# Strassen's output layer: its sums and low halves moved from GpSimd to VectorE, in wider pieces, with the products in another order

## Chip, core and metric

The kernel runs on one core of one Trainium2 chip. The metric is the device time of one execution in microseconds (us), the median of several runs; less is better. An execution lasts 1.85 us longer than the span of its trace, which goes from the first to the last instruction.

## What is computed

Attention over 4 batches of 12 heads, 448 tokens and 64 dimensions, then a gated layer and a cosine layer, each followed by a matrix product. All inputs are float32.

```python
x = attention(q, k, v, g_q, g_k)               # 1792 tokens x 768
g = x @ w_gate                                 # 768 x 1536
x = (silu(g) * (x @ w_val)) @ w_out            # 1536 x 768
h = x @ w2_in                                  # 768 x 2048
out = (h * cos(h)) @ w2_out                    # 2048 x 768: the output layer
```

The change is in the last line's product, and in what prepares its weights.

## The kernel before

**Precision.** An fp32 factor is held as two float16 halves, high and low (the low half is the value less the high one), and a product of two such factors is three matmuls: high by high, high by low, low by high (`mm_out`).

**The output layer** multiplies A (1792 tokens by 2048) by w2_out with one level of Strassen's scheme in Winograd's form: seven products of blocks of half the tokens, half the inner dimension and half the columns, in place of eight. The inner half is cut in eight chunks c of 128 rows. `A[c]` is a tile with four places of 896 columns: A11 and A12 as float16 pairs, A21 and A22 as fp32 (`f32_of(c, 2)` and `f32_of(c, 3)`). The products also take sums of blocks: S3 = A11 - A21, S2 = A22 - S3, S4 = A12 - S2, S1 = A21 + A22. A product goes over four `runs`, each with two chunks and seven token tiles of 128, six matmuls of 128x384 for each tile and run: 42 matmuls in a run, 28 runs in the layer. The seven tiles lie in seven of eight PSUM banks, and products that share a sum go on accumulating in the same banks (a chain). `o_fin` takes a finished tile out of PSUM, scaled.

**The sums of blocks** are emitted behind each run for its two chunks: `s_32` (S3 into tiles of its own, S2 in A11's place, behind A11's run), `s_4` (S4 in A12's place, behind A12's), `s_22` (A22 split into halves in A11's place, behind S2's) and `s_1` (behind S3's). Each does 448 columns at a time. VectorE does the sums, ScalarE the high half (`put`), GpSimd the low half and one difference in `s_4`.

**The weights** of the layer are w2_out's blocks and their sums T. `pre_step` loads w2_out, turns it and stores it as `o32`. `t_step` loads a chunk of `o32` into a `raw` tile, does four subtractions of 384 columns on GpSimd and stores the result as `oT`; it is called late in the cosine layer (from chunk 5, batch 3) and at the output layer's start. `o_load` loads two chunks' weights for a run, `o_split` makes their halves (ScalarE the high one, VectorE the low one).

**The cosine layer** before it (called h here) has 8 chunks by 4 batches, 36 matmuls of 128x448 each; `fin_h` makes A's blocks of them, on VectorE and ScalarE with a small subtraction on GpSimd. Before h comes the gated layer's second product (out1), with `pre_step` beside it.

**Order.** All DMAs are issued from SyncE's queue (SP). Each engine works its own queue in order. A scheduler sets the order in these queues when the kernel is built; it moves an instruction of one part between those of another.

## Time and profile before

| | us |
|---|---|
| median of 3 runs (1327.07 to 1330.24) | 1329.25 |
| the profiled execution | 1329.15 |
| its span | 1327.3 |
| TensorE busy | 1182.5 |
| VectorE busy | 981.9 |
| ScalarE busy | 691.6 |
| GpSimd busy | 547.1 |

Busy times are sums over the whole span. Stages have different limits, so a stage is read by the busy time within it and by what each engine waited for there. A busy TensorE is not a TensorE at its peak: matmuls overlap, so a matmul's own duration is about twice the step from one to the next.

### The profile page before, as it was taken

What the parts mean: (1) busy time and instruction counts of PE and PEld (TensorE: products, weight loads), DVE (VectorE), ACT (ScalarE), POOL (GpSimd) and SP (SyncE); (2) the same over time, 40 slices, a digit from 0 to 9 for tenths busy, and PEclk for the clock granted to TensorE, in tenths of its full rate; (3) what the DMA queues carried; (4) which work ended last, traced back from release to release, by engine and by line L of the source; (5) the groups of instructions that cost most, each with busy time, mean ns of one, the idle gap of its engine ahead of it and who ended that gap; (6) DMA issues with size and microseconds to landing.
All of it is one profiled execution on the core that took longest, in us unless ns stands there. A gap on an engine that the chain in (4) does not pass through costs nothing. (4 is left out here: it accounts for less than half of the span.)

```text
span 1327.3 us, 18341 instructions
## 1 busy us (share of the span) xinstructions
PE 1182.5 (89%) x6292; PEld 661.4 (50%) x6292; DVE 981.9 (74%) x1760; ACT 691.6 (52%) x1342; POOL 547.1 (41%) x437
## 2 busy tenths in 40 slices
PE   1887988998999989999999999999999886648998
PEld 0332333444764459544586548555555443325665
DVE  5987866798779992478644986677788799989531
ACT  3675655544666544556643453577776554335210
POOL 7753402534324452145540125122215478889400
PEclk9898989998999999999999999999999998869999
DMA  5655666459877797787576977501123761121222
GB/s 147 173 149 134 184 170 178 99 162 253 240 213 188 224 234 232 186 212 188 123 232 227 307 284 260 170 0 48 48 72 127 256 236 60 36 65 49 72 67 71
DMA packets 220782, 211.54 MB, mean 159 GB/s; under 512 B 147601, under 2 KB 178193, under 8 KB 220689
## 3 DMA queue, kind: packets, MB, share of 16 engines
q1 hardware_dynamic: 220688, 210.38, 54.7%
q8 instruction: 49, 0.80, 0.3%
q14 instruction: 45, 0.36, 0.1%
HBM read 138.44 MB, written 41.57 MB: 136 GB/s over the span
## 5 line engine op out<-in xcount | busy, mean ns | idle before, releaser
L163 PE MATMUL mm<-xy,wp 128*128 128x448 f16 x2484 | 493.5, 355 | 6.3 <-DVE ga L1128 3.2
L163 PEld LDWEIGHTS <-wp 128*128 128x128 f16 x2880 | 278.4, 99 | 280.5 <-issue 36.6
L163 PE MATMUL mm<-g,wp 128*128 128x448 f32 x864 | 183.1, 369 | 1.6 <-DVE ga L1136 1.6
L163 POOL TENSOR_TENSOR g<-tmp,g 128x224 f16<-128x224 f32 (+1 forms) x112 | 112.1, 1010 | 159.1 <-ACT g L1257 154.5
L163 PEld LDWEIGHTS mm<-g,wp 128*128 128x128 f32 x864 | 160.6, 188 | 19.7 <-issue 4.4
L163 PEld LDWEIGHTS <-g 128*128 128x128 f16 x1008 | 99.9, 99 | 94.8 <-issue 27.2
L163 POOL TENSOR_TENSOR g<-ga,g 128x448 fp32r<-128x448 f32 x48 | 64.5, 1357 | 145.4 <-ACT g L1138 145.3
L507 ACT ACTIVATE pr<-s,sm,esc 128x448 f32<-128x448 f32 x84 | 60.3, 718 | 80.2 <-DVE sm L501 73.7
L163 PE MATMUL s<-T 128*64 128x448 f16 x336 | 63.8, 398 | 39.6 <-DVE T L666 21.6
L163 POOL TENSOR_TENSOR wp<-w,wp 128x768 fp32r<-128x768 f32 x36 | 72.3, 2011 | 60.5 <-ACT wp L1024 40.3
L163 PE MATMUL s<-wp,g 128*128 128x384 f16 x432 | 78.7, 338 | 14.6 <-ACT u L1361 9.7
L935 DVE TENSOR_SCALAR w<-raw 128x768 int32<-128x768 int32 x68 | 48.5, 716 | 53.1 <-POOL wp L163 19.4
L163 PE MATMUL mm<-wp,g 128*128 128x384 f16 x432 | 75.4, 327 | 10.5 <-DVE g L1253 4.3
L163 PEld LDWEIGHTS <-T 128*64 128x64 f16 (+1 forms) x432 | 28.8, 109 | 110.2 <-issue 83.6
L163 POOL TENSOR_TENSOR ri<-ss,half 128x14 f32<-128x14 f32 x24 | 64.1, 2672 | 37.9 <-DVE ss L356 36.3
L497 DVE TENSOR_REDUCE sm<-s 128x1 f32<-128x448 f32 x84 | 51.2, 615 | 36.4 <-PE s L163 36.3
L163 POOL TENSOR_TENSOR p<-pr,p 128x448 f16<-128x448 f32 x36 | 41.1, 1149 | 88.6 <-ACT p L531 70.5
L1342 DVE SCALAR_TENSOR_TENSOR wp<-w,oscl,wp 128x384 f16<-128x384 f32 x56 | 54.7, 1001 | 29.8 <-ACT wp L1341 29.7
L937 DVE SCALAR_TENSOR_TENSOR w<-raw,w 128x768 int32<-128x768 int32 x68 | 74.9, 1101 | 0.6
L936 DVE SCALAR_TENSOR_TENSOR w<-raw,w 128x768 int32<-128x768 int32 x68 | 74.1, 1093 | 0.6
L163 POOL TENSOR_TENSOR xy<-tmp,xy 128x448 f16<-128x448 f32 x24 | 27.8, 1160 | 110.2 <-ACT xy L774 83.4
L955 ACT ACTIVATE raw<-w 128x768 f32<-128x768 f32 x56 | 46.9, 838 | 47.6 <-DVE w L937 34.4
(199 smaller groups left out, 2108.3 us busy)
## 6 DMA issues: line engine op xcount, KB each, us to landing
raw<-in_moe_w_out_dram SPq DMA_DIRECT2D x28, 768.0 KB, 5.3
raw<-in_moe_w_in_dram SPq DMA_DIRECT2D x16, 768.0 KB, 5.5
raw<-in_moe_w_gate_dram SPq DMA_DIRECT2D x12, 768.0 KB, 6.2
raw<-in_moe_w_val_dram SPq DMA_DIRECT2D x12, 768.0 KB, 5.8
wp<-scr_gate SPq DMA_DIRECT2D x24, 384.0 KB, 4.5
w<-scr_out SPq DMA_DIRECT2D x24, 384.0 KB, 3.9
wp<-scr_val SPq DMA_DIRECT2D x24, 384.0 KB, 5.0
y<-tmp SPq DMA_DIRECT2D x30, 224.0 KB, 3.9
```

The source lines that it names most:

```text
L163: r = f(*args, **kw)
L497: nc.vector.tensor_reduce(sm[:, 0, t:t + 1], slot[n][:, :S], axis=AX.X, op=ALU.max)
L507: nc.scalar.activation(e, slot.pop(n)[:, :S], AF.Exp, bias=sm[:, 1, t:t + 1], scale=esc, accum_out=sm[:, 2, t:t + 1],)
L935: nc.vector.tensor_scalar(wi, hi, 3, 0x3FFFFFF8, op0=ALU.logical_shift_left, op1=ALU.bitwise_and)
L936: nc.vector.scalar_tensor_tensor(wi, hi, -0x40000000, wi, op0=ALU.bitwise_and, op1=ALU.bitwise_or)
L937: nc.vector.scalar_tensor_tensor(wi, lo, 29, wi, op0=ALU.logical_shift_right, op1=ALU.bitwise_or)
L955: nc.scalar.activation(sq_dst[0], w32, AF.Square, accum_out=n[:, 0:1])
L1342: nc.vector.scalar_tensor_tensor(wp[:, i, 1], w, so, wp[:, i, 0], op0=ALU.mult, op1=ALU.subtract)
```

## The change

Sums and low halves of the output layer go to VectorE, in pieces of 896 columns where their temporaries allow it (these are now `raw` tiles, two of them). S1's sum is taken in `s_4` and lands in A21's place. `s_1` follows S2's run. The products come in the order A11, A12, S3, S2, A22, S1, S4, with A22 in a chain of its own, and `o_fin` adds the results up in another way. `t_step` also goes to VectorE; it begins in the gated layer's second product (from visit `TSTEP` on), where it uses four small `yt` tiles, so its load and its store are four DMAs each of 192 KB, and it goes on in h, in a `raw` tile, with one load and four stores.

```diff
@@ -42,6 +42,7 @@
 NPH = 3
 EARLY = 75
 PREL = 33
+TSTEP = 25
 HPRE = (5, 3)
 LO = 3
 WL = 8
@@ -1044,18 +1045,25 @@
     t_new = []
     t_in = []
 
-    def t_step():
+    def t_step(more=True, small=None):
 
         if t_in:
             c, t = t_in.pop()
             for d, x, y in ((0, 1, 0), (1, 3, 1), (3, 3, 0), (2, 2, 3)):
-                gps.tensor_sub(t[:, d], t[:, x], t[:, y])
-            stores.append((oT[c].rearrange("p m f -> p (m f)"), t.rearrange("p m f -> p (m f)")))
-        if t_new:
+                nc.vector.tensor_sub(t[d], t[x], t[y])
+            stores.extend((oT[c][:, i], t[i]) for i in range(4))
+        if t_new and more:
             c = t_new.pop(0)
-            t = rot("raw").tile([P, 6 * 256], I32, tag="raw", name="raw").bitcast(F32)
-            sync.dma_start(t, o32[c].rearrange("p m f -> p (m f)"))
-            t_in.append((c, t.rearrange("p (m f) -> p m f", f=CO)))
+            w_store()
+            if small is None:
+                t = rot("raw").tile([P, 6 * 256], I32, tag="raw", name="raw").bitcast(F32)
+                sync.dma_start(t, o32[c].rearrange("p m f -> p (m f)"))
+                t = [t[:, i * CO:(i + 1) * CO] for i in range(4)]
+            else:
+                t = [small.tile([P, S], F32, tag="yt", name="yt")[:, :CO] for _ in range(4)]
+                for i in range(4):
+                    sync.dma_start(t[i], o32[c][:, i])
+            t_in.append((c, t))
         return bool(t_in or t_new)
 
     def pre_step(more=True):
@@ -1272,53 +1280,54 @@
 
     def put(dst, src):
         nc.scalar.activation(dst[0], src, AF.Copy)
-        gps.tensor_sub(dst[1], src, dst[0])
-
-    def pair(c, i, k):
+        nc.vector.tensor_sub(dst[1], src, dst[0])
+
+    def pair(c, i, k=slice(0, TS)):
         return A[c][:, i, 0, k], A[c][:, i, 1, k]
+
+    def wide_tmp():
+        return rot("raw").tile([P, 6 * 256], I32, tag="raw", name="raw").bitcast(F32)[:, :TS]
 
     def s_32(c):
 
         tt = nc.vector.tensor_tensor
         S3[c] = [s3_pool[0].tile([P, TS], F16, tag="s3", name="s3") for _ in range(2)]
-        for k in HALVES:
-            hi, lo = pair(c, 0, k)
-            s3, s2 = tmp(), tmp()
-            tt(s3, hi, f32_of(c, 2)[:, k], op=ALU.subtract)
-            tt(s3, s3, lo, op=ALU.add)
-            put([x[:, k] for x in S3[c]], s3)
-            tt(s2, f32_of(c, 3)[:, k], s3, op=ALU.subtract)
-            put((hi, lo), s2)
+        hi, lo = pair(c, 0)
+        s3, s2 = wide_tmp(), wide_tmp()
+        tt(s3, hi, f32_of(c, 2), op=ALU.subtract)
+        tt(s3, s3, lo, op=ALU.add)
+        nc.scalar.activation(S3[c][0], s3, AF.Copy)
+        tt(s2, f32_of(c, 3), s3, op=ALU.subtract)
+        nc.scalar.activation(hi, s2, AF.Copy)
+        tt(S3[c][1], s3, S3[c][0], op=ALU.subtract)
+        tt(lo, s2, hi, op=ALU.subtract)
 
     def s_4(c):
 
+        tt = nc.vector.tensor_tensor
         for k in HALVES:
             (h1, l1), (h2, l2) = pair(c, 1, k), pair(c, 0, k)
             s4, u = tmp(), tmp()
-            nc.vector.tensor_tensor(s4, h1, h2, op=ALU.subtract)
-            gps.tensor_sub(u, l1, l2)
-            nc.vector.tensor_tensor(s4, s4, u, op=ALU.add)
+            tt(s4, h1, h2, op=ALU.subtract)
+            tt(u, l1, l2, op=ALU.subtract)
+            tt(s4, s4, u, op=ALU.add)
             put((h1, l1), s4)
+        tt(f32_of(c, 2), f32_of(c, 2), f32_of(c, 3), op=ALU.add)
 
     def s_22(c):
 
-        for k in HALVES:
-            put(pair(c, 0, k), f32_of(c, 3)[:, k])
+        put(pair(c, 0), f32_of(c, 3))
 
     def s_1(c):
 
-        s1 = [tmp(), tmp()]
-        for k, t in zip(HALVES, s1):
-            nc.vector.tensor_tensor(t, f32_of(c, 2)[:, k], f32_of(c, 3)[:, k], op=ALU.add)
-        for k, t in zip(HALVES, s1):
-            put(pair(c, 3, k), t)
+        put(pair(c, 3), f32_of(c, 2))
 
     s3_pool = []
     u_pool = []
     out_w = {}
     out_wp = {}
 
-    CHAINS = ((("A11", 0), ("A12", 2)), (("S2", 7), ("S3", 5), ("A22", 6)), (("S1", 4), ("S4", 3)))
+    CHAINS = ((("A11", 0), ("A12", 2)), (("S3", 5), ("S2", 7)), (("A22", 6),), (("S1", 4), ("S4", 3)))
     PLACE = {"A11": 0, "S2": 0, "A22": 0, "A12": 1, "S4": 1, "S1": 3}
     runs = [
         dict(x=x, w=w, c=c, chain=r, first=k == 0 and c == 0, last=c + 2 == NH, k=k)
@@ -1347,35 +1356,35 @@
             return lambda a: S3[c][a][:, cols]
         return lambda a: A[c][:, PLACE[rn["x"]], a, cols]
 
-    P1 = {}
+    U3 = {}
     U2 = {}
-    U3 = {}
 
     def o_fin(rn, t, ps):
         e, b = (t + 1) * P, t * P // SH
         ci = osc[:, b:b + 1] if e <= (b + 1) * SH else osc[:, B + b:B + b + 1]
         ps = ps[:, :CO]
         chain, k = rn["chain"], rn["k"]
+        stt = nc.vector.scalar_tensor_tensor
         if chain == 0 and k == 0:
-            P1[t] = u_pool[0].tile([P, CO], F32, tag="u", name="u")
-            nc.scalar.activation(P1[t], ps, AF.Copy, scale=ci)
+            U3[t] = u_pool[0].tile([P, CO], F32, tag="u", name="u")
+            nc.scalar.activation(U3[t], ps, AF.Copy, scale=ci)
             return
-        if chain == 1 and k < 2:
-            if k == 0:
-                if t % 4 == 0:
-                    U2[None] = rot("raw").tile([P, 6 * 256], I32, tag="raw", name="raw").bitcast(F32)
-                d = U2[t] = U2[None][:, t % 4 * CO:(t % 4 + 1) * CO]
-            else:
-                d = U3[t] = S3[t % 6][t // 6].bitcast(F32)[:, :CO]
-            nc.vector.scalar_tensor_tensor(d, ps, ci, P1[t], op0=ALU.mult, op1=ALU.add)
+        if chain == 1 and k == 0:
+            if t % 4 == 0:
+                U2[None] = rot("raw").tile([P, 6 * 256], I32, tag="raw", name="raw").bitcast(F32)
+            U2[t] = U2[None][:, t % 4 * CO:(t % 4 + 1) * CO]
+            nc.scalar.activation(U2[t], ps, AF.Copy, scale=ci)
+            return
+        if chain == 1:
+            stt(U3[t], ps, ci, U3[t], op0=ALU.mult, op1=ALU.add)
+            nc.vector.tensor_sub(U2[t], U3[t], U2[t])
             return
         o = tmp()[:, :CO]
         if chain == 0:
             nc.scalar.activation(o, ps, AF.Copy, scale=ci)
         else:
-            add = P1[t] if chain == 1 else (U3, U2)[k][t]
-            nc.vector.scalar_tensor_tensor(o, ps, ci, add, op0=ALU.mult, op1=ALU.add)
-        h, f = ((0, 0), (1, 0), (1 - k, 1))[chain]
+            stt(o, ps, ci, (U3, U2)[k][t], op0=ALU.mult, op1=ALU.add)
+        h, f = ((0, 0), (1, 0), (1 - k, 1))[max(chain - 1, 0)]
 
         def store():
             for b in range(B):
@@ -1485,6 +1494,8 @@
                 w_loads(j + (WL if j + WL < 2 * KX else LA))
             if bn == B and qn % 2 == 0:
                 pre_step(qn < PREL)
+            if bn == B and qn >= TSTEP:
+                t_step(True, y_pool[0])
             for it in sched.get(qn, ()):
                 if bn < B:
                     step(it, bn)
@@ -1516,6 +1527,8 @@
 
     while pre_step(False):
         w_store()
+    w_store()
+    t_step(False)
     w_store()
     g_ctx.close()
     more_ctx.close()
@@ -1563,13 +1576,15 @@
                 late.append((0, fin))
             else:
                 fin()
+    while t_step():
+        w_store()
+    w_store()
     xy_ctx.close()
     s3_pool.append(ctx.enter_context(tc.tile_pool(name="s3", bufs=2 * NH)))
     u_pool.append(ctx.enter_context(tc.tile_pool(name="u", bufs=TS // P)))
     seq = 0
     ps = {}
     for j, rn in enumerate(runs):
-        t_step()
         w_store()
         o_load(j + 2)
         o_split(j + 1)
@@ -1584,7 +1599,7 @@
             while len(deferred) > (1 if rn["last"] else 0):
                 deferred.pop(0)()
         for c in (rn["c"], rn["c"] + 1):
-            for x, f in (("A11", s_32), ("A12", s_4), ("S2", s_22), ("S3", s_1)):
+            for x, f in (("A11", s_32), ("A12", s_4), ("S2", s_22), ("S2", s_1)):
                 if rn["x"] == x:
                     f(c)
     for f in deferred:
```

Line numbers move by one to nineteen, so a helper's line L163 is L164 in the changed kernel, and L1342 is L1351. What the scheduler makes of it is shown at three places.

VectorE's queue ahead of the product that uses S3. Before the change (S3's product is the second of its chain there), these rows make S3 and S2 of chunk 2: L1287 and L1288 are S3's sum, L1290 is S2's, L1342 makes a low half of a weight; `g_9109` is the tile A of chunk 2.

```order
L1288 TENSOR_TENSOR tmp<-tmp,g_8841 128x448
L1342 SCALAR_TENSOR_TENSOR wp<-w_11185,oscl,wp 128x384
L1290 TENSOR_TENSOR tmp<-g_8841,tmp 128x448
L1287 TENSOR_TENSOR tmp<-g_9109 128x448
L1342 SCALAR_TENSOR_TENSOR wp<-w_11263,oscl,wp 128x384 x2
L1288 TENSOR_TENSOR tmp<-tmp,g_9109 128x448
L1290 TENSOR_TENSOR tmp<-g_9109,tmp 128x448
```

Of the change, eleven rows of the same queue: L1300 and L1302 (S2's sum, S3's low half) of chunk 4, whose A is `g_9737` and whose S3 halves are `s_11059` and `s_11060`; L1297 and L1298 (S3's sum) of chunk 5, A `g_10011`; L1313, L1311, L1283 and L1303 belong to S4 of chunks 3 and 4 and to S2's low half of chunk 4.

```order
L1300 TENSOR_TENSOR raw<-g_9737,raw 128x896
L1302 TENSOR_TENSOR s_11060<-raw,s_11059 128x896
L1313 TENSOR_TENSOR tmp<-tmp 128x448
L1351 SCALAR_TENSOR_TENSOR wp<-w_11668,oscl,wp 128x384 x2
L1313 TENSOR_TENSOR tmp<-tmp 128x448
L1297 TENSOR_TENSOR raw<-g_10011 128x896
L1303 TENSOR_TENSOR g_9737<-raw,g_9737 128x896
L1311 TENSOR_TENSOR tmp<-g_9737 128x448
L1283 TENSOR_TENSOR g_9463<-tmp,g_9463 128x448 x2
L1298 TENSOR_TENSOR raw<-raw,g_10011 128x896
L1315 TENSOR_TENSOR g_10011<-g_10011 128x896
```

S3's low half now stands in VectorE's queue, 896 columns wide, and between the low halves of two chunks stand the pieces of S4 of the chunks before.

TensorE's queue where the third product begins in the change. `mm<-wp,s_10915` is a matmul with S3's high half of chunk 0; `s_11059` and `s_11060` are the halves of chunk 4, `s_11070` and `s_11071` those of chunk 5. The first PSUM bank takes six chunks in a row, and only then comes the second bank (`s<-wp`).

```order
L164 MATMUL mm<-wp,s_11059 128x384
L164 LDWEIGHTS s_11060
L164 MATMUL mm<-wp,s_11060 128x384
L164 LDWEIGHTS s_11070
L164 MATMUL mm<-wp,s_11070 128x384
...
L164 LDWEIGHTS s_11071
L164 MATMUL mm<-wp,s_11071 128x384
L164 LDWEIGHTS s_10915
L164 MATMUL s<-wp,s_10915 128x384
```

Before the change the second chain's first bank takes S2 of the chunks, in A's own tiles (`g_10221` and `g_10561` are chunks 6 and 7), ahead of S3 (`s_10861`, chunk 0):

```order
L163 LDWEIGHTS g_10221
L163 MATMUL mm<-wp,g_10221 128x384
...
L163 LDWEIGHTS g_10561
L163 MATMUL mm<-wp,g_10561 128x384
...
L163 LDWEIGHTS s_10861
L163 MATMUL mm<-wp,s_10861 128x384
```

So the chain's first bank asked for S2 of all eight chunks before, and now asks for S3 of six.

SP's queue in out1, where `w_8072<-scr_out` and the like load out1's weights, `o_1`, `o_2`, `o_3` and `oT_175` to `oT_177` are chunks of `o32` and `oT`. Before:

```order
L163 DMA o_2_169<-w_7995 128x768
L163 DMA raw<-in_moe_w_out_dram 128x1536
L163 DMA w_8072<-scr_out_0_9_146 128x768
L163 DMA w_8114<-scr_out_1_0_129 128x768
L163 DMA o_2_169<-w_8081 128x768
L163 DMA raw<-in_moe_w_out_dram 128x1536
L163 DMA w_8138<-scr_out_1_3_130 128x768
L163 DMA o_3_170<-w_8147 128x768
L163 DMA w_8178<-scr_out_1_6_147 128x768
```

Of the change:

```order
L164 DMA w_8072<-scr_out_0_9_146 128x768
L164 DMA w_8114<-scr_out_1_0_129 128x768
L164 DMA yt<-o_1_168 128x384
L164 DMA o_2_169<-w_8081 128x768
L164 DMA yt<-o_2_169 128x384 x2
L164 DMA raw<-in_moe_w_out_dram 128x1536
L164 DMA oT_176<-yt 128x384
L164 DMA w_8146<-scr_out_1_3_130 128x768
L164 DMA oT_176<-yt 128x384
L164 DMA yt<-o_2_169 128x384
L164 DMA oT_176<-yt 128x384
L164 DMA w_8202<-scr_out_1_6_147 128x768
```

Stores of `oT` and loads of `yt` from `o32` now stand between the loads of out1's weights, and a load of `o_2` stands right behind the store that fills it.

## Rows read from the trace of the kernel before

**Rows 1.** The page: span, and busy tenths in 40 slices of 33.2 us.

```profile
span 1327.3 us, 18341 instructions
...
PE   1887988998999989999999999999999886648998
...
POOL 7753402534324452145540125122215478889400
```

**Rows 2.** Output layer by windows: busy us (instructions) of each engine, granted TensorE clock, DMA.

```profile
1072.00:1241.00 169.00, 118.22 (x671) 67.51 (x669) 158.91 (x158) 75.79 (x144) 144.88 (x112) 0.86 0.24 80
1241.00:1324.00 83.00, 82.69 (x509) 49.59 (x507) 24.03 (x42) 7.85 (x14) 0.08 (x1) 1.00 0.22 69
...
1150.00:1180.00 30.00, 4.73 (x15) 1.81 (x14) 29.79 (x28) 7.79 (x14) 26.10 (x20) 0.54 0.13 39
```

**Rows 3.** TensorE's waits in the output layer: total, times, longest.

```profile
PE mm L163 <- ACT g L1274: 21.4, 1, 21.4
PE s L163 <- ACT u L1361: 9.7, 2, 9.5
...
PE mm L163 <- DVE g L1253: 4.3, 2, 2.5
```

**Rows 4.** TensorE's timeline: the output layer's first row, an undisturbed run, the last row.

```profile
1072.05 3.09 PE L163 MATMUL s<-wp,g 128*128 128x384 f16 x18
...
1249.42 3.09 PE L163 MATMUL s<-wp,g 128*128 128x384 f16 x18
...
1256.25 3.09 PE L163 MATMUL s<-wp,g 128*128 128x384 f16 x18
...
1322.55 1.14 PE L163 MATMUL mm<-wp,g 128*128 128x384 f16 x6
```

**Rows 5.** ScalarE's timeline in TensorE's longest wait: its puts wait for VectorE.

```profile
1164.73 0.58 ACT L1274 ACTIVATE g<-tmp 128x448 f16<-128x448 f32 x1 [4.77 <-DVE tmp L1300]
```

**Rows 6.** VectorE and GpSimd together, 1106 to 1110 us.

```profile
1106.21 1.30 POOL L163 TENSOR_TENSOR raw<-raw 128x384 f32<-128x384 f32 x1
1106.59 1.41 DVE L1288 TENSOR_TENSOR tmp<-tmp,g 128x448 f32<-128x448 f32 x1
1108.10 0.62 DVE L1290 TENSOR_TENSOR tmp<-g,tmp 128x448 f32<-128x448 f32 x1
1108.64 0.62 DVE L1287 TENSOR_TENSOR tmp<-g 128x448 f32<-128x448 f16 x1
1108.68 1.47 POOL L163 TENSOR_TENSOR s<-tmp,s 128x448 f16<-128x448 f32 x1 [1.17 <-ACT s L1274]
1109.30 1.33 DVE L1288 TENSOR_TENSOR tmp<-tmp,g 128x448 f32<-128x448 f32 x1
```

**Rows 7.** A 896-column product of two tensors in the attention stage (ns, min/median/max).

```profile
L410 DVE TENSOR_TENSOR rqk<-rqk,ri x12: 1030/1401/2016, 212.1 to 603.0; 128x896 f32<-128x896 f32 x12
```

**Rows 8.** Weight splits: mean in the output layer, and a pair with GpSimd idle.

```profile
L1342 DVE SCALAR_TENSOR_TENSOR wp<-w,oscl,wp 128x384 f16<-128x384 f32 x52 | 50.3, 989 | 29.8 <-ACT wp L1341 29.7
...
1256.17 1.15 DVE L1342 SCALAR_TENSOR_TENSOR wp<-w,oscl,wp 128x384 f16<-128x384 f32 x2 [5.72 <-ACT wp L1341]
```

**Rows 9.** VectorE at the seam of h and the output layer: parts of fin_h.

```profile
1073.64 1.26 DVE L1248 SCALAR_TENSOR_TENSOR tmp<-tmp,ht,mm 128x448 f32<-128x448 int32 x2
...
1090.86 0.38 DVE L1253 SCALAR_TENSOR_TENSOR g<-tmp,mm 128x224 f32<-128x224 f32 x1
```

**Rows 10.** TensorE's waits late in h, 1030 to 1072 us.

```profile
PE s L163 <- ACT raw L955: 5.0, 3, 2.4
```

**Rows 11.** Out1: a window as in rows 2, TensorE at a norm, SP, a DMA's landing time.

```profile
820.00:880.00 60.00, 57.41 (x298) 37.75 (x297) 38.19 (x83) 33.78 (x64) 11.94 (x10) 1.00 0.42 139
...
834.92 0.38 PE L163 MATMUL s<-nm,full 128*128 128x1 f32 x2 [1.67 <-ACT raw L955]
...
800.82 0.32 SPq L163 DMA_DIRECT2D o<-w  x1
801.84 0.33 SPq L163 DMA_DIRECT2D raw<-in_moe_w_out_dram  x1
...
o<-w SPq DMA_DIRECT2D x16, 384.0 KB, 3.8
```

## The prediction

> **What bounds the kernel now.** I read the slices of the page first. TensorE is at nine tenths nearly everywhere, and drops to six and four tenths in three slices near the end, where GpSimd is at eight and nine [rows 1]. Those slices are the output layer, so the windows of that stretch come next. From 1072 to 1241 us VectorE is busy 158.9 of 169 us, GpSimd 144.9, ScalarE 75.8; from 1241 on TensorE runs alone at the full clock (1.00) [rows 2]. The list of TensorE's waits says for whom it waits: 21.4 us in one piece for a `put` of ScalarE, 9.7 for an eviction by ScalarE, 4.3 for the last pieces of `fin_h` on VectorE [rows 3]. ScalarE itself waits in that time for VectorE, 4.77 us ahead of one put [rows 5]. So the sums on VectorE set the end of this layer, with ScalarE's queue standing behind them.
>
> The size of the prize: an undisturbed run of 42 matmuls takes 1256.25 - 1249.42 = 6.83 us [rows 4]. The layer has 28 runs, 191.2 us. It took from 1072.05 to 1322.55 + 1.14 = 1323.69, which is 251.6 us [rows 4]. So 60.4 us is lost there, and no more than that can be won in it.
>
> **Price of a sum on VectorE.** One operation has two prices in the trace. A 448-column sum takes 1.41 and 1.33 us where GpSimd works, and 0.62 where GpSimd stands idle, between 1107.51 and 1108.68 us; two of the short ones start 0.54 us apart [rows 6]. The changed layer has no GpSimd instruction, so I take the short price: 0.60 for a step of 448 columns, between the 0.54 of independent ones and 0.66 (1109.30 - 1108.64) of one that needs the one before it. For 896 columns the trace has one operation, in the attention stage: 1.03 us at best, 2.02 at worst [rows 7]. I take 1.05, with bounds of 0.99 (twice 0.54, less the second start, about 0.09) and 1.10. A weight split costs 1.15 / 2 = 0.575 with GpSimd idle, and 0.99 on average now [rows 8].
>
> [...]
>
> **The output layer after.** Let t0 be its first matmul, as 1072.05 is now. VectorE first has to finish h. Now it begins the last two `fin_h` at 1073.64 and ends them at 1091.24 [rows 9], 19.2 us after t0. In the changed order the same stretch has 16 pieces of `fin_h` (8 x 0.6 + 8 x 0.3), 12 splits (6.9) and five 896-column sums (5.25), 20 us with small ones. Begun when the data is there (6.2 us ahead of t0) it ends at t0 + 14, begun as late as now at t0 + 21.6. I take 17.
>
> Then VectorE has to reach the low half of S3 of chunk 7, the last thing that the third product needs. By then its queue holds 39 operations of 896 columns (of `s_32` 5 x 8, less the last one and six that stand earlier, and the sums for S1 of six chunks), 52 of 448 columns (`s_4` of six chunks, eight each, and four of the seventh) and 18 splits: 39 x 1.05 + 52 x 0.60 + 18 x 0.575 = 82.5 us. That is t0 + 99.5. The pieces of S4 stand ahead of S3 in the queue, though their product is the last one: 31 us of the 82.5.
>
> TensorE is through A11 and A12, eight runs, at t0 + 54.6. S3's first bank asks for six chunks in a row, and chunk 5's low half comes after 59 of the 82.5 us, at t0 + 76. So TensorE stands some 20 us at S3's start, again 4 us for chunk 7, and ends S3 at 99.5 + 6.8 = t0 + 106.3. A12's evictions on ScalarE queue behind puts that wait for VectorE, within the same 20 us. Such a wait brings the clock down, as the 0.54 of 1150 to 1180 us shows [rows 2]; the 4 us of slack ahead of chunk 7 take the slow matmuls up. After that VectorE has 60 us of work left (17 operations of 896 columns, 12 of 448, 61 of 384), so the last four products run through: 4 x 27.3 = 109.2, end at t0 + 215.5. Against 251.6 that is **36.1 us less**. Bounds: prices low and high give 75.7 and 88.4 in place of 82.5 (-6.8, +5.9), the seam -3 and +4.6.
>
> **Late in h.** TensorE waits 5.0 us there for norms of w2_out's last rows, which come late through two `raw` tiles [rows 10]. `t_step` holds these tiles for fewer rounds (three of eight chunks are left in h) and shorter (four subtractions at 0.575 are 2.3 us). Gain between 0 and 5.0; I take **2.5 us less**. The twelve subtractions there cost VectorE 6.9 us; the cover is GpSimd's silence, which shortens VectorE's other work.
>
> **Out1.** Five chunks of `t_step` go here: 20 subtractions, 11.5 us of VectorE, which has 21.8 of 60 us free [rows 11]. That costs nothing. Their DMAs do: a load of `o_2` stands in SP's queue right behind the store that fills it, and holds the queue until that has landed, 3.8 us. Behind it stand the next `raw` load and out1's weights; now a `raw` load follows such a store after 1.0 us. A late `raw` load makes a late norm, and TensorE already waits 1.67 us at one [rows 11]. Four such rounds in out1, 0 to 3.5 us each: 0 to 14. Near the low end, since loads run ahead by two pieces: I take **5 us more**.
>
> Sum: 1327.3 - 36.1 - 2.5 + 5 = 1293.7 us of span, and the 1.85 us outside it: 1295.5, say 1295. The profiled execution (1329.15) is the median (1329.25) within 0.1 us, so it is the same for both.
>
> **Rivals.**
> 1. Out1's weights wait behind the new DMAs: 14 us in place of 5, 1304. For it: SP's order. Against it: out1's DMA share is 0.42 [rows 11].
> 2. VectorE waits inside its own queue. S3's low half needs ScalarE's high half, and ScalarE's queue has puts into A12's place that wait until A12's run is through. Now VectorE stands idle 169 - 158.9 = 10 us there [rows 2]; so much again gives 1305.
> 3. TensorE gets its S3 earlier: low prices (-6.8), seam at its best (-3), all of h's 5.0 and nothing lost in out1 (-7.5): 1278.
> 4. Slower: the long price is not GpSimd's doing, and VectorE with more work keeps it. 39 x 2.02 + 52 x 1.33 + 18 x 0.99 = 166 us in place of 82.5, 1379. It decides from a mean price 1.4 times the short one, 0.85 us for 448 columns, where the 33.6 us are gone. Against it: both short sums in the middle of long ones, just where GpSimd is idle [rows 6].
>
> **How the numbers follow.** The forecast 0.52 (its own range 1287 to 1304, from prices and seam), rival 1 0.16, rival 2 0.14, rival 3 0.12, rival 4 0.06. A measurement of this kernel tells 0.2% (2.7 us) from no change. All but rival 4 are faster; of its 0.06 I give 0.02 to no change, where the price is near the deciding one. For 8 in 10 the range reaches from near rival 3, 1280, to rivals 1 and 2 with the high prices, 1305 + 6 = 1311.
>
> **What would show it.** In the changed profile: no GpSimd in the output layer; 448 columns near 0.62 us and 896 near 1.08; one wait of TensorE near 20 us at S3's start, for a low half on VectorE or an eviction behind it; none after S3; 215 us from the layer's first matmul to its last. In out1, waits of TensorE for ScalarE's squares of some 5 us. I am wrong if the sums stay at 1.2 us and more, if out1 or h gains or loses over 10 us, or if S3 is not where TensorE waits.

## The result, and the profile after

The changed kernel takes 1290.03 us, the median of four runs (1286.67 to 1296.36), against 1328.16 of the kernel before: a ratio of 0.972, 95% interval 0.968 to 0.976. The prediction was 1295. One of e1's ten executions below took 1526.75 us, at a mean clock of 0.75, and is left out of e1's figures.

The profiled execution is the slowest of the four, 1296.36 us with a span of 1294.6. In it the last matmul of attention starts at 687.3 us, in the kernel before at 682.7, and in the runs below between 680.2 and 685.5. So some 4.6 us of this execution were lost ahead of the stages that the change touches. Two rows of a view by tile, the kernel before and then the changed one (count, ns min/median/max, first and last start):

```profile
L163 PE MATMUL t<-PT,vl x96: 352/353/581, 278.7 to 682.7; 128*64 128x448 f16 x72, 64*64 64x448 f16 x24
```
```profile
L164 PE MATMUL t<-PT,vl x96: 352/353/581, 283.7 to 687.3; 128*64 128x448 f16 x72, 64*64 64x448 f16 x24
```

TensorE's timeline of the changed kernel (as in [rows 4]; in brackets the idle time ahead and what ended it) shows the layer's first row, a wait of 1.9 us for the first weights' split, the four waits at S3's start and the last row. With t0 = 1075.92 the layer ends at 1289.49 + 1.14 = 1290.63, after 214.7 us where it took 251.6.

```profile
1075.92 0.65 PE L164 MATMUL s<-wp,g 128*128 128x384 f16 x3
...
1078.65 1.62 PE L164 MATMUL s<-wp,g 128*128 128x384 f16 x9 [1.92 <-DVE wp L1351]
...
1138.16 0.34 PE L164 MATMUL mm<-wp,s 128*128 128x384 f16 x1 [3.13 <-DVE s L1302]
1145.89 0.82 PE L164 MATMUL mm<-wp,s 128*128 128x384 f16 x2 [7.39 <-ACT s L1299]
1149.52 0.50 PE L164 MATMUL mm<-wp,s 128*128 128x384 f16 x1 [2.81 <-DVE s L1302]
1154.33 7.93 PE L164 MATMUL s<-wp,s 128*128 128x384 f16 x32 [4.31 <-ACT tmp L1384]
...
1289.49 1.14 PE L164 MATMUL t<-wp,g 128*128 128x384 f16 x6
```

Late in h one norm is waited for, 1.2 us, where [rows 10] have 5.0 (list of waits from 1030 us on):

```profile
PE s L164 <- ACT raw L956: 1.2, 1, 1.2
```

In the timeline, L1299 and L1302 are the high and the low half of S3, L1384 is A12's eviction. The four are 17.6 us together, and behind 1154.33 TensorE waits for nothing more. That eviction had itself waited 2.6 us on ScalarE for a low half of S4 (L1283), as the profile has it: both use the pool of six `tmp` tiles, and S4's low half is the last to read one of them.

```profile
1153.70 1.06 ACT L1384 ACTIVATE tmp<-s,osc 128x384 f32<-128x384 f32 x2 [2.56 <-DVE g L1283]
```

The windows say the same (columns as in [rows 2]): VectorE is busy without a gap from 1120 to 1150, GpSimd does nothing, and the granted clock is down at 0.82 and 0.84 where TensorE stood before and between its matmuls. In windows of half a microsecond it is 0.50 from 1139.5 to 1159.5 us, and 1.00 from 1124 to 1139 and from 1160 to 1164.

```profile
1120.00:1150.00 30.00, 16.67 (x97) 9.10 (x96) 30.00 (x44) 10.25 (x15) 0.00 (x0) 0.82 0.17 53
1150.00:1180.00 30.00, 25.69 (x144) 14.72 (x143) 29.58 (x44) 16.55 (x29) 0.00 (x0) 0.84 0.24 74
1180.00:1210.00 30.00, 30.00 (x186) 18.07 (x185) 20.34 (x28) 18.49 (x28) 0.00 (x0) 1.00 0.20 64
```

VectorE's timeline beside [rows 6]: 448 columns last 0.61 us and start 0.54 apart, 896 last 1.07 and start 1.00 apart, one after the other without a gap. The first row is the end of `fin_h`, the last two are the low halves of chunks 5 and 7.

```profile
1093.46 0.37 DVE L1261 SCALAR_TENSOR_TENSOR g<-tmp,mm 128x224 f32<-128x224 f32 x1
...
1120.00 0.61 DVE L1312 TENSOR_TENSOR tmp<-g 128x448 f32<-128x448 f16 x1
1120.54 0.61 DVE L1311 TENSOR_TENSOR tmp<-g 128x448 f32<-128x448 f16 x1
1121.07 0.61 DVE L1312 TENSOR_TENSOR tmp<-g 128x448 f32<-128x448 f16 x1
1121.61 1.07 DVE L1298 TENSOR_TENSOR raw<-raw,g 128x896 f32<-128x896 f32 x1
1122.61 1.07 DVE L1315 TENSOR_TENSOR g<-g 128x896 f32<-128x896 f32 x1
...
1148.38 1.08 DVE L1302 TENSOR_TENSOR s<-raw,s 128x896 f16<-128x896 f32 x1
...
1170.03 1.08 DVE L1302 TENSOR_TENSOR s<-raw,s 128x896 f16<-128x896 f32 x1
```

For the stages ahead of the layer, windows that start 100 and 310 us behind attention's last matmul, of the kernel before and of the changed one. The first row of each is out1 and the start of h, where TensorE gets 461 matmuls done in place of 482, at a clock of 0.97 in place of 1.00; the second is the end of h, 423 in place of 394.

```profile
782.70:882.70 100.00, 94.18 (x482) 66.03 (x481) 66.32 (x131) 53.83 (x100) 34.17 (x24) 1.00 0.50 168
992.70:1072.70 80.00, 75.02 (x394) 38.99 (x393) 67.03 (x143) 51.35 (x99) 41.40 (x42) 0.98 0.55 192
```
```profile
787.30:887.30 100.00, 93.27 (x461) 66.66 (x460) 77.74 (x138) 47.70 (x87) 32.55 (x20) 0.97 0.74 250
997.30:1077.30 80.00, 78.24 (x423) 41.46 (x422) 70.56 (x164) 54.23 (x105) 16.63 (x22) 1.00 0.43 148
```

### The profile page after: what moved, and what is told of

It is laid out like the page before. It is cut to its first block, busy times and chain, and to the rows that moved or that the text cites. A ratio compares the mean times of both kernels' runs of the same rounds, so it can differ in the third digit from the quotient of the medians.

```text
span 1294.6 us, 18256 instructions
## 1 busy us (share of the span) xinstructions
PE 1176.9 (91%) x6292; PEld 661.0 (51%) x6292; DVE 966.6 (75%) x1824; ACT 689.0 (53%) x1317; POOL 389.4 (30%) x309
## 5 line engine op out<-in xcount | busy, mean ns | idle before, releaser
L164 PE MATMUL mm<-xy,wp 128*128 128x448 f16 x2484 | 490.2, 354 | 5.5 <-DVE ga L1136 3.0
L164 PEld LDWEIGHTS <-wp 128*128 128x128 f16 x2880 | 277.1, 99 | 277.0 <-issue 32.1
L164 PE MATMUL mm<-g,wp 128*128 128x448 f32 x864 | 188.1, 375 | 5.2 <-DVE ga L1144 2.5
L164 PEld LDWEIGHTS mm<-g,wp 128*128 128x128 f32 x864 | 163.1, 191 | 25.5 <-issue 4.4
L164 PEld LDWEIGHTS <-g 128*128 128x128 f16 x1008 | 98.6, 98 | 67.4 <-issue 2.3
L164 POOL TENSOR_TENSOR g<-tmp,g 128x224 f16<-128x224 f32 x64 | 54.3, 856 | 191.7 <-ACT g L1265 191.2
L164 POOL TENSOR_TENSOR g<-ga,g 128x448 fp32r<-128x448 f32 x48 | 65.2, 1372 | 145.3 <-ACT g L1146 145.0
L164 PE MATMUL s<-T 128*64 128x448 f16 x336 | 64.1, 401 | 43.2 <-DVE T L667 23.5
L164 POOL TENSOR_TENSOR wp<-w,wp 128x768 fp32r<-128x768 f32 x36 | 71.8, 2000 | 67.1 <-ACT wp L1025 41.4
L164 PEld LDWEIGHTS <-T 128*64 128x64 f16 (+1 forms) x432 | 28.5, 109 | 113.8 <-issue 84.5
L164 PE MATMUL s<-wp,g 128*128 128x384 f16 x432 | 74.9, 326 | 1.9 <-DVE wp L1351 1.9
L164 POOL TENSOR_TENSOR ri<-ss,half 128x14 f32<-128x14 f32 x24 | 64.1, 2670 | 39.1 <-DVE ss L357 37.7
L164 PE MATMUL mm<-wp,g 128*128 128x384 f16 x432 | 74.6, 326 | 0.0
L938 DVE SCALAR_TENSOR_TENSOR w<-raw,w 128x768 int32<-128x768 int32 x68 | 73.3, 1078 | 0.5
L937 DVE SCALAR_TENSOR_TENSOR w<-raw,w 128x768 int32<-128x768 int32 x68 | 72.0, 1061 | 0.5
L164 POOL TENSOR_TENSOR p<-pr,p 128x448 f16<-128x448 f32 x36 | 41.9, 1170 | 88.9 <-ACT p L532 69.1
L164 POOL TENSOR_TENSOR xy<-tmp,xy 128x448 f16<-128x448 f32 x24 | 28.3, 1179 | 112.2 <-ACT xy L775 73.4
L713 ACT ACTIVATE pr<-c,esc 128x448 f32<-128x448 f32 x84 | 50.0, 626 | 19.8 <-PE c L164 19.7
## 6 DMA issues: line engine op xcount, KB each, us to landing
y<-tmp SPq DMA_DIRECT2D x30, 224.0 KB, 4.2
```

The source lines that it names most:

```text
L164: r = f(*args, **kw)
L713: nc.scalar.activation(e, ps[:, :S], AF.Exp, scale=esc)
L937: nc.vector.scalar_tensor_tensor(wi, hi, -0x40000000, wi, op0=ALU.bitwise_and, op1=ALU.bitwise_or)
L938: nc.vector.scalar_tensor_tensor(wi, lo, 29, wi, op0=ALU.logical_shift_right, op1=ALU.bitwise_or)
```

## The experiments

Theory: VectorE's sums were long because GpSimd worked beside them, and with short sums the layer ends when VectorE has worked through its queue up to S3's last low half. Rivals: the long price has another cause; the order of the products won the time; the wide pieces did.

All twelve in one table. "Layer" is from its first matmul to the end of its last, in the profiled run. Ratios are to the kernel before on the same chip (medians 1329 to 1332).

| run | us | ratio, 95% interval | layer |
|---|---|---|---|
| e1 `t_step` alone | 1321.1 | 0.995 (0.993 to 0.997) | 245.6 |
| e2 old order | 1300.6 | 0.980 (0.976 to 0.983) | 224.0 |
| e3 low halves on GpSimd | 1313.9 | 0.989 (0.987 to 0.992) | 235.2 |
| e4 GpSimd beside | 1319.9 | 0.994 (0.991 to 0.996) | 243.7 |
| e5 `s_32` in halves | 1304.7 | 0.981 (0.980 to 0.983) | 229.4 |
| e6 `s_4` behind S3 | 1269.6 | 0.955 (0.953 to 0.956) | 191.7 |
| e7 A22 apart | 1270.5 | 0.956 (0.953 to 0.958) | 193.3 |
| e8 halves, `s_4` late | 1282.9 | 0.965 (0.963 to 0.966) | 204.7 |
| e9 `t_step` in h only | 1282.0 | 0.964 (0.962 to 0.967) | 201.4 |
| e10 GpSimd narrow | 1304.2 | one run | 228.3 |
| e11 e8, run by run | 1284.3 | 0.966 (0.963 to 0.970) | 207.1 |
| e12 changed, run by run | 1293.5 | 0.973 (0.970 to 0.976) | 214.6 |

**The change taken apart: e1 and e2.** e1 is the kernel before with the `t_step` part of the diff alone.

> The kernel before with one part of the change alone: t_step on VectorE, begun in out1 with small tiles, and none of it left in the output layer. By the count of matmuls in the two traces this part costs some 5 us in out1 (the prediction: 5) and gives back some 6 late in h (the prediction: 2.5). The output layer, with 10 subtractions of 1.24 us fewer on GpSimd, gains 0 to 5 us. Together 1322 to 1329 us, against 1328 before. Rival: out1 loses no time from it and the lag seen there was a late start of the one profiled execution; then 1317 to 1323. Second rival: what out1 loses is not given back in h, which gained from something else; then 1330 to 1334.

It won 7 to 8 us (the ratio and the medians), a little more than expected, and 6.0 of it in the output layer (245.6 for 251.6), where ten subtractions of GpSimd are gone. The time lies in the first rival's range, but not by its mechanism: in the window of out1 TensorE gets 456 matmuls done, where 482 were before. From attention's last matmul to the layer's first it took 390.7 us, against 389.4 before and 388.6 in the changed kernel: what out1 loses, the end of h gives back, but for some 1 us either way.

e2 is the changed kernel with the old order (and with it `o_fin` and the place of `s_1` as before):

```diff
-    CHAINS = ((("A11", 0), ("A12", 2)), (("S3", 5), ("S2", 7)), (("A22", 6),), (("S1", 4), ("S4", 3)))
+    CHAINS = ((("A11", 0), ("A12", 2)), (("S2", 7), ("S3", 5), ("A22", 6)), (("S1", 4), ("S4", 3)))
```

> The changed kernel with the products, the chains and o_fin in the order of before (S2, S3, A22 in one chain; s_1 behind S3). Theory: the time came from the price of a sum on VectorE, and the order as such is worth little: S2's low half stands one 896-column operation (1.08 us) behind S3's in VectorE's queue, so TensorE stands some 20 us at S2's start in place of S3's, and the time is 1288 to 1297 us. Rival: the order itself won 10 us or more, by giving VectorE less to do ahead of the third product; then 1300 us and more, with a second long wait of TensorE behind the first.

My theory fell here: the order is worth some 10 us. TensorE has a second wait, 8.6 us at the start of the second product of the chain:

```profile
1183.51 4.73 PE L164 MATMUL mm<-wp,s 128*128 128x384 f16 x20 [8.61 <-DVE raw L1379]
```
```profile
1180.85 2.08 DVE L1283 TENSOR_TENSOR g<-g 128x896 f16<-128x896 f32 x2
1182.85 0.60 DVE L1379 SCALAR_TENSOR_TENSOR raw<-mm,osc,u 128x384 f32<-128x384 f32 x1
```

S3's matmuls need banks that hold S2, and L1379 is S2's eviction. In the old order it adds to another tile, on VectorE, and stands there behind low halves of A22 (L1283), which only the chain's third product wants. In the changed order the first product of that chain is taken out by ScalarE. Taken in these steps, the 38 us are some 8 for `t_step`, 20 for the sums on VectorE in wide pieces, and 10 for the order.

**Whose doing is the long price: e3, e4 and e10.** e3 puts the low halves back on GpSimd, with order and widths as changed.

```diff
     def put(dst, src):
-        nc.vector.tensor_sub(dst[1], src, dst[0])
+        gps.tensor_sub(dst[1], src, dst[0])
...
-            tt(u, l1, l2, op=ALU.subtract)
+            gps.tensor_sub(u, l1, l2)
...
-        tt(S3[c][1], s3, S3[c][0], op=ALU.subtract)
-        tt(lo, s2, hi, op=ALU.subtract)
+        gps.tensor_sub(S3[c][1], s3, S3[c][0])
+        gps.tensor_sub(lo, s2, hi)
```

> The changed kernel with the low halves and the difference of low halves in s_4 on GpSimd again, the order and the widths as changed. If GpSimd's work makes VectorE's operations long: 24 of 896 columns at 2.0, 26 of 448 at 1.35 and 18 splits at 1.0 are 101 us in place of the 82.5 ahead of S3's last low half, so some 18 us later: 1304 to 1312 us, 448 columns at 1.3 us on VectorE and 896 near 2. If the long price is not GpSimd's doing (rival 4), VectorE keeps 0.61 and 1.08 here with 40 operations fewer, and the time is 1290 us or less.

24 us slower than the changed kernel, 2 us more than my range, although VectorE has fewer operations. They are long again. Two groups of sums, one of each width, on VectorE from 1070 to 1240 us (busy us, mean ns); the other groups of 896 columns have means of 1.2 to 1.7 us:

```profile
L1313 DVE TENSOR_TENSOR tmp<-tmp 128x448 f32<-128x448 f32 x16 | 19.7, 1245 | 0.0
L1297 DVE TENSOR_TENSOR raw<-g 128x896 f32<-128x896 f16 x7 | 14.3, 2042 | 0.0
```

e4 changes no engine's work; it adds 40 subtractions on GpSimd that nobody reads.

```diff
...
+    gps.tensor_copy(dm[:, 0], f32_of(NH - 1, 2)[:, HALVES[1]])
+    for i in range(DUMMY):
+        gps.tensor_sub(dm[:, 1], dm[:, 0], dm[:, 0])
```

> The changed kernel with 40 subtractions of 448 fp32 columns added on GpSimd, on a tile of their own that nothing else reads, from the end of h's last block on. They change no other engine's work and nobody waits for them. At the 1.36 us that such a one takes before, they last 55 us. If GpSimd's work alone makes VectorE's operations long, those in this stretch take 1.3 us (448) and 2.0 (896) and the ones behind it 0.61 and 1.08 again; VectorE does 27 us less in the 55, TensorE stands 40 us and more at S3's start, and the time is 1308 to 1322 us. If the long price has another cause, nothing changes: 1287 to 1297.

It cost 30 us, 29.0 of it in the layer. VectorE's timeline of e4, in the middle of that stretch, and GpSimd's:

```profile
1101.86 1.81 DVE L1298 TENSOR_TENSOR raw<-g 128x896 f32<-128x896 f16 x1
1103.60 1.35 DVE L1314 TENSOR_TENSOR tmp<-tmp 128x448 f32<-128x448 f32 x1
1104.87 1.82 DVE L1304 TENSOR_TENSOR g<-raw,g 128x896 f16<-128x896 f32 x1
```
```profile
1092.31 53.65 POOL L165 TENSOR_TENSOR dm<-dm 128x448 f32<-128x448 f32 x39
```

A step of 896 columns takes 1103.60 - 1101.86 = 1.74 us, one of 448 takes 1.27: both 0.74 more than alone. VectorE starts 38 operations beside these 39, and 39 x 0.74 is 28.9 us, which is the layer's loss. So GpSimd's work makes VectorE's operations long by itself, and rival 4 is out. e10 makes e4's operations on GpSimd half as wide.

```diff
-        gps.tensor_sub(dm[:, 1], dm[:, 0], dm[:, 0])
+        gps.tensor_sub(dm[:, 1, :SH], dm[:, 0, :SH], dm[:, 0, :SH])
```

> The changed kernel with 40 subtractions of 224 columns beside it on GpSimd, in place of 448. With 448 each operation of VectorE took 0.73 us longer, one of 448 columns and one of 896 alike. If each of them waits for one whole operation of GpSimd, half as wide a one makes it some 0.35 to 0.45 us: 0.9 to 1.0 us from start to start for 448 columns, 1.35 to 1.45 for 896. If the two engines share a rate instead, the width of GpSimd's operations doesn't matter: 1.27 and 1.74 again. The stretch is then shorter, so the time lies between the changed kernel's 1290 and the 1320 of the wide ones.

```profile
1098.79 1.44 DVE L1298 TENSOR_TENSOR raw<-g 128x896 f32<-128x896 f16 x1
1100.15 0.98 DVE L1314 TENSOR_TENSOR tmp<-tmp 128x448 f32<-128x448 f32 x1
1101.05 1.44 DVE L1304 TENSOR_TENSOR g<-raw,g 128x896 f16<-128x896 f32 x1
```

Now 1.36 and 0.90: 0.36 us more than alone, for both widths, and 39 x 0.36 is 14.0 us, where the layer takes 13.6 longer than the changed one's. What a sum of VectorE pays goes by the width of GpSimd's operation, half as much for half the width, and not by its own width.

**What TensorE waits for at S3: e6, e7 and e12.** e6 emits `s_4` later, and nothing else:

```diff
-            for x, f in (("A11", s_32), ("A12", s_4), ("S2", s_22), ("S2", s_1)):
+            for x, f in (("A11", s_32), ("S3", s_4), ("S2", s_22), ("S2", s_1)):
```

> The changed kernel with s_4 emitted behind S3's runs in place of A12's, nothing else. If TensorE's 17.6 us at S3's start are S4's pieces standing ahead of S3's in VectorE's queue (some 28 us of it), that wait goes whole: S3's last low half is then there near t0 + 50 to 60 and TensorE asks for it from t0 + 54.6 on. The layer ends at t0 + 193 to 200 in place of 214.7, and the time is 1269 to 1277 us. Rival: the stall only moves, since VectorE now does S4's pieces while S3 and S2 run and A22's halves queue behind them; then TensorE waits 10 us and more at A22's start and the time is 1280 or more.

The wait went whole, and the layer takes 1264.04 + 1.14 - 1073.44 = 191.7 us, where 28 undisturbed runs are 191.2:

```profile
1073.44 0.65 PE L164 MATMUL s<-wp,g 128*128 128x384 f16 x3
...
1264.04 1.14 PE L164 MATMUL t<-wp,g 128*128 128x384 f16 x6
```
```profile
1120.00:1150.00 30.00, 30.00 (x187) 18.04 (x186) 29.97 (x43) 14.84 (x25) 0.00 (x0) 1.00 0.32 99
1150.00:1180.00 30.00, 30.00 (x186) 18.07 (x185) 30.00 (x51) 21.40 (x36) 0.00 (x0) 1.00 0.18 53
```

VectorE is as busy as before, but on what is wanted next, and the clock stays at 1.00. Chunk 5's low half of S3 comes at t0 + 50.9 in place of 73.5, before TensorE is through with A12 (t0 + 54.6). Part of my working was off: S3's last low half, chunk 7's, comes at t0 + 72, not 50 to 60. It is in time because the scheduler now has TensorE take S3 run by run, so that it asks for chunk 7 near t0 + 76. This kernel is faster than both: 0.955.

e7 goes on from there, with A22's halves in S3's place, so that nothing can queue up in front of A22 (`o_x` reads A22 there).

```diff
-        put(pair(c, 0), f32_of(c, 3))
+        put(S3[c], f32_of(c, 3))
...
-            for x, f in (("A11", s_32), ("A12", s_4), ("S2", s_22), ("S2", s_1)):
+            for x, f in (("A11", s_32), ("S3", s_22), ("S2", s_4), ("S2", s_1)):
```

> As the kernel with s_4 behind S3's runs, and A22's halves put where S3 lay (as soon as an S3 run is through with its chunks) in place of where S2 lies, so that S4 can wait until behind S2's runs: s_22 behind S3's runs, s_4 and s_1 behind S2's. VectorE then has 28 us less ahead of S3's last low half, 8 operations of 1 us ahead of A22, and S4's pieces are wanted last (t0 + 164). If the queue order on VectorE was all that stood between the layer and its floor of 191.2 us, no wait over 2 us is left: t0 + 193 to 196, 1266 to 1273 us. Rival: ScalarE, which now has the puts of A22 and S1 early, holds A12's evictions or S3's high halves back; then a wait of 5 us and more for ScalarE at S3's start and 1276 or more.

As expected, and no better than e6: there was nothing left to win. e12 asks whether TensorE's order alone makes the wait.

```diff
+    in_order.add("PE")
     seq = 0
     ps = {}
```

> The changed kernel with TensorE's instructions of the output layer in the order in which they are written, nothing else. VectorE ended S3's low halves of chunks 5, 6 and 7 at t0 + 73.5, 83.8 and 95.2 in the changed kernel, with S4's pieces between them. Run by run TensorE asks for chunk 5 at t0 + 70 and for chunk 7 at t0 + 80. If S4's pieces ahead of S3's on VectorE make the wait, it is still there, a later one of 12 to 16 us before chunk 7, and S3 ends near t0 + 102: 1284 to 1291 us, little or nothing won. Rival: TensorE's order alone made the wait (the first token tile through six chunks in a row); then it goes and the time is 1268 to 1277.

It doesn't: the layer stays at 214.6 us, and the time is 2 us above my range. The waits for S3's halves are gone, and in their place TensorE stands for A12's eviction, which is in ScalarE's queue behind puts that wait for VectorE and then waits 2.6 us for a low half of S4, as in the changed kernel; and 6.1 us for the last `fin_h`.

```profile
1087.28 2.08 PE L164 MATMUL mm<-wp,g 128*128 128x384 f16 x6 [6.09 <-DVE g L1261]
1150.48 4.67 PE L164 MATMUL s<-wp,s 128*128 128x384 f16 x18 [10.86 <-ACT tmp L1384]
```

I had expected the wait before chunk 7; it came earlier, at the eviction. What TensorE gained in order it lost to the same queue on VectorE.

**The width by itself: e5, e8 and e11.** e5 has `s_32` in halves on `tmp` tiles, as in the kernel before, but on VectorE.

```diff
-        hi, lo = pair(c, 0)
-        s3, s2 = wide_tmp(), wide_tmp()
-        tt(s3, hi, f32_of(c, 2), op=ALU.subtract)
+        for k in HALVES:
+            hi, lo = pair(c, 0, k)
+            s3, s2 = tmp(), tmp()
+            tt(s3, hi, f32_of(c, 2)[:, k], op=ALU.subtract)
...
```

> The changed kernel with s_32 in pieces of 448 columns in place of 896, all still on VectorE. With GpSimd silent, two steps of 0.54 us stand for one of 1.00, so 48 operations become 96 and VectorE's queue ahead of S3's last low half grows by some 3 us; it is busy without a gap there, so TensorE waits as much longer: 1291 to 1296 us, near no difference from the changed kernel's 1290. Rival: the wide pieces are what won time, also without GpSimd beside them; then 1300 us and more. Second rival: shorter pieces let ScalarE's high halves overlap better, and S3 comes earlier: below 1288.

The first rival has the time, 15 us slower, but not through the width itself. S3's low halves came sooner (chunk 7 at t0 + 74, in place of 95), but A12's evictions stand behind ten puts of S4 in ScalarE's queue, and the first of them then waits for a low half of S4 (L1283), which frees a `tmp` tile. TensorE's timeline, and ScalarE's with the last of these puts and the eviction:

```profile
1165.52 8.70 PE L164 MATMUL s<-wp,s 128*128 128x384 f16 x35 [21.61 <-ACT tmp L1385]
```
```profile
1161.67 0.58 ACT L1282 ACTIVATE g<-tmp 128x448 f16<-128x448 f32 x1 [2.10 <-DVE tmp L1314]
1163.28 0.58 ACT L1282 ACTIVATE g<-tmp 128x448 f16<-128x448 f32 x1 [1.03 <-DVE tmp L1314]
1164.88 0.58 ACT L1385 ACTIVATE tmp<-s,osc 128x384 f32<-128x384 f32 x1 [1.03 <-DVE g L1283]
```

e8 joins e5 and e6.

> Both edits together: s_32 in pieces of 448 columns, and s_4 behind S3's runs. In the run with the pieces alone S3's low halves came some 10 us sooner, and TensorE then stood 21.6 us for A12's eviction, which lay in ScalarE's queue behind ten puts of S4 that each wait for VectorE. If that is all that the pieces cost, it goes with S4's pieces behind S3: no wait over 2 us, 1268 to 1275 us, as with wide pieces. Rival: the pieces hold the six tmp tiles that A12's evictions need too, whatever the place of s_4; then a wait of 5 us and more for an eviction, and 1277 or more.

The time, 1282.9 us, is in the rival's range, but no eviction of A12 is waited for. The 21.6 us are gone, and TensorE waits 7.7 us in four pieces at S3's start, where it takes the first token tile through all eight chunks in a row. e11 adds e12's line.

> Pieces of 448 columns and s_4 behind S3's runs, and TensorE's instructions of the output layer kept in the order in which they are written: run by run, all seven token tiles of chunks 0 and 1 before chunk 2. In the run without this TensorE took the first token tile through all eight chunks first, so it asked for chunk 7 at t0 + 70 where the wide pieces' kernel asked at t0 + 75, and for chunk 2 to 6 much earlier; VectorE's last low half of S3 came at t0 + 72 in both. If this order is what the narrow pieces cost, the waits at S3's start go (no more than 2 us is left of 7.7) and the time is 1268 to 1273 us. Rival: ScalarE's twice as many high halves, each a step behind VectorE, cost it; then 1279 to 1284 again.

The rival had the time. The waits for S3 went, but A12's eviction is 6.1 us late, behind S3's high halves on ScalarE, and at the layer's start TensorE waits 5.3 us for the last `fin_h`. So the two orders of TensorE cost about the same here, each by another wait, and S4's place alone is not all of e6: S3's halves and A12's evictions must both be in time, as they are there. Whether narrow pieces cost nothing with the evictions moved ahead on ScalarE was not tried.

**`t_step`'s place: e9.** e6 with all of `t_step` at the end of h.

```diff
-TSTEP = 25
+TSTEP = 999
```

> The kernel with s_4 behind S3's runs (1269.6 us, no wait of TensorE in the output layer, so what comes before it shows in full), and t_step kept out of out1: all eight chunks late in h. If t_step's DMAs cost out1 some 4 us and give back as much late in h, through shorter waits for norms, the two go together and the time is the same within 2 us: 1268 to 1272. Rival one: out1's loss is real and h's gain is only GpSimd's silence there; then 1264 to 1267. Rival two: out1 lost nothing and eight chunks late in h hold the raw tiles as before; then 1272 to 1277.

12 us slower than e6, beyond the second rival's range. Windows of e6 and of e9 that start 100 us and 310 us behind attention's last matmul, and e9's first rows in the layer:

```profile
781.50:881.50 100.00, 92.82 (x460) 66.42 (x459) 78.42 (x138) 47.08 (x86) 32.60 (x20) 0.97 0.74 252
...
991.50:1068.10 76.60, 74.71 (x395) 39.11 (x394) 66.02 (x148) 50.42 (x98) 15.97 (x20) 0.98 0.43 150
```
```profile
782.50:882.50 100.00, 94.38 (x485) 66.24 (x484) 66.70 (x131) 54.79 (x100) 34.29 (x24) 1.00 0.51 172
...
992.50:1069.10 76.60, 73.35 (x393) 38.25 (x392) 67.11 (x147) 48.75 (x94) 14.93 (x20) 1.00 0.60 209
```
```profile
1061.76 7.35 PE L164 MATMUL mm<-xy,wp 128*128 128x448 f16 x38
1075.12 1.12 PE L164 MATMUL s<-wp,g 128*128 128x384 f16 x3 [6.01 <-ACT wp L1350]
```

Out1 gets its 25 matmuls back (some 5 us), and the end of h does nearly as many as e6's, 393 and 395, with six of the eight rounds in it, about as many as the kernel before has there. The loss comes behind it: the other two rounds fall around and into the output layer, its first weights are 6.0 us late, and it is 9.7 us longer, 5.7 of them waits at S3. So five chunks in out1 cost some 5 us and save some 16.

## Why the prediction was right

| step | predicted | measured |
|---|---|---|
| 448 columns, 896, a split | 0.60, 1.05, 0.575 | 0.54, 1.00, 0.53 from start to start |
| VectorE done with h | t0 + 17 | t0 + 17.8 |
| chunk 5's low half of S3 | t0 + 76 | t0 + 73.5 |
| chunk 7's | t0 + 99.5 | t0 + 95.2 |
| TensorE's wait at S3 | 20 and 4 us | 17.6 us, none later |
| layer | 215.5 | 214.7 |
| out1 | +5 | +4.4 |
| late h | -2.5 | -5.5 |

**Prices and queue.** The count of operations was right, and the prices were 5 to 12% too high: I had set them between the distance of two starts and the duration, and the distance is what counts. With it the sum is 39 x 1.00 + 52 x 0.535 + 18 x 0.53 = 76.4 us, and 17.8 + 76.4 is t0 + 94.2, against the 95.2 measured. Most of the last 1.0 us goes to three operations beside GpSimd's last subtraction of `fin_h`, which ends at t0 + 20.8 (their steps are 1.07, 1.34 and 0.95 us in place of 1.00, 1.00 and 0.54); the prediction had GpSimd silent in the whole layer. Its bounds of 75.7 and 88.4 us come out with 0.54 and 0.66 for 448 columns only if a split is 0.50 and 0.62, for which it gave no row; with 0.575 they are 77.0 and 87.6. The 0.09 us of the second start had no row either; the changed run has 2 x 0.54 - 1.00 = 0.08. In VectorE's timeline above each sum starts before the end of the one ahead (1122.61 - 1121.61 = 1.00 us behind a duration of 1.07).

**The wait.** It stood where the prediction put it, and the two things that end it, a low half on VectorE and an eviction on ScalarE behind it, are both in it; the longest of the four pieces ends with a high half on ScalarE, which had waited for VectorE in its turn. The second wait, for chunk 7, did not come, so chunk 7's low half did not set the layer's end as I had it: it was there 4.3 us earlier than predicted, and the layer ended only 0.8 us earlier. What I had set off against that wait, the slower clock, cost some 4 us instead: 191.2 + 1.9 (the first weights' split) + 17.6 is 210.7, of 214.7. That the layer's sum fits to 0.8 us is in part luck, since these errors cancel. e6 shows the cause of the wait: with S4's pieces behind S3's, wait and slow clock both go, and e12 shows that TensorE's order alone doesn't do it.

**Out1** had the right size by luck, since the mechanism was another. I had SP's queue held by loads of `o_2` behind their stores, and late norms behind that. That wait is not among SP's any more; SP waits 10.4 us for the subtractions themselves, ahead of the stores of `oT` (its list from 785 to 865 us):

```profile
SPq L164 <- DVE yt L1053: 10.4, 7, 4.2
```

TensorE's waits rose little (5.8 to 6.7 us idle in the window), and those for norms fell, from 4.8 to 4.0 us; most of the loss goes with the clock, 0.97 for 1.00, as in e1 and e6 too, and not in e9 (1.00). What brought the clock down stays open: it is 0.83 in two stretches of 10 us, with waits of up to 1.6 us in or ahead of them, and stays at 1.00 around the 1.67 us of [rows 11].

**Late in h** is the term that was mis-sized: 29 matmuls more in 80 us are 5.5 us, where I took half of the 5.0 us of norm waits. These fell to 1.2 us, and the clock rose from 0.98 to 1.00. I had put the gain down to fewer rounds and shorter ones. e9 has about as many rounds there as the kernel before, and does 393 matmuls where that does 376 in as long a window. So most of it is VectorE in GpSimd's place; fewer rounds take a part of the norm waits, which are 3.2 us in e9 and 1.8 in e6. How the rest divides between shorter holds of the `raw` tiles and GpSimd's silence was not tried apart. Late h (3.0 us), the layer (0.8) and out1 (0.6) are together most of what the median lies below the prediction. The profiled execution lies at the predicted time only because it began 4.6 us late: 1327.3 - 0.7 (out1 and h) - 36.9 (layer) + 4.6 is 1294.3, of 1294.6.

**Rivals.** The first, 14 us in out1, is out by the window (4.4 us), and the fourth, another cause of the long price, by e3, e4 and e10. The second had VectorE wait inside its own queue, and VectorE is busy 59.6 of the 60 us from 1120 to 1180, so it is out; that in-order queues wait on each other shows on ScalarE instead, in the 4.3 us for A12's eviction, and in full in e5 (21.6 us) and e12 (10.9). Of the third, lower prices and all of h's gain came, but the prices brought the layer's end only 0.8 us.

## What to carry to other kernels

An engine that is busy without a gap can still be late (VectorE, busy 59.6 of 60 us, while TensorE stood 17.6 for what it makes): look at what stands in its queue ahead of the work that is wanted next. Here moving the sums off GpSimd, in wide pieces, won some 20 us, and one word that put S4's sums behind S3's product, which does not need them, won 20 more. When a piece's width or place is changed, look at all queues again, the one that empties PSUM first: an eviction behind puts that wait for another engine cost as much (21.6 us in e5) as the sums had. Look also at the tiles that such an eviction shares with other work.

## What the runs showed of the hardware

A sum of VectorE, with two inputs, pays for GpSimd by the operation, not by the column: 0.74 us beside subtractions of 448 columns (e4) and 0.36 beside 224 (e10), for 448 and for 896 columns alike. So the same sums in wider pieces lose less to a busy GpSimd: in e4 one of 896 columns loses 0.74 us, and two of 448 lose 1.48. GpSimd's own operations then last 1.38 us (53.65 / 39), about as long as VectorE's mean step there (53.65 / 38 = 1.41), and 38 operations of VectorE stand beside GpSimd's 39 (in e10 39 beside 39). That is what two engines that take turns would show; whether they do, and for how much of an operation, no run here tells.
